# Attention and feed-forward on one core: early queries and keys loaded with two heads side by side, and the first sixteen weight loads cut in four

## The chip, the core and the metric

The kernel runs on one core of one Trainium2 chip. A core has TensorE (PE in the profile, PEld for its weight loads), VectorE (DVE), ScalarE (ACT), GpSimd (POOL) and SyncE (SP), each with an instruction queue of its own that is worked off in order. SyncE and, in a few places, ScalarE issue transfers (DMA) between the chip's memory and the core's SBUF. The metric is device time of one execution in microseconds.

## The reference

Eight batches of eight heads, 576 positions of 64 numbers each. Heads 0 to 3 look at the last 32 positions ("local"), heads 4 to 7 at every 32nd earlier position ("strided"). The attention's output goes through a feed-forward part with a gate.

```python
scores = scale * np.matmul(q, k.transpose(0, 1, 3, 2))
mask_local = (rel >= 0) & (rel < 32)
mask_strided = (rel >= 0) & (pos[None, :] % 32 == pos[:, None] % 32)
# softmax of the masked scores over the last axis
attn_out = np.matmul(attn, v)
x = attn_out.transpose(0, 2, 1, 3).reshape(4608, 512)
h = x @ w_in                                  # 512 x 2048
g = h * np.clip(h + 3.0, 0.0, 6.0) / 6.0
out = g @ w_out                               # 2048 x 512
```

Queries, keys and values are 32-bit floats, the two weight matrices 64-bit.

## The kernel before

The work is cut into tiles of 512 tokens, one for each batch `b`. Attention goes by pairs of heads: `pair(g)` does pair `c` of batch `b`, where pairs 0 and 1 are local and 2 and 3 strided; in the first batch the order is 0, 2, 1, 3. A pair has these steps: load queries and keys; turn them so that the 64 numbers of a head lie on the partitions (two heads on 128); scores in PSUM; mask, maximum, exponential, sum and division on the other engines; turn the result; multiply it with the values; copy it out as two parts of the tile's `x`. Then `ffn(b)` runs the two products of the feed-forward part, with each matrix split into a high and a low part, so that each product is three.

All of this is not issued as it is written. Each step is given to `op(engine, us, ...)` with a supposed duration, the data it reads and writes and a due time, and `Plan.emit` plays the steps through with these durations and writes the engines' instructions in the order that comes out. The durations are the planner's own numbers; a change to one moves instructions in the whole program. For loads, `after` is the time that the planner lets each take of the transfer's time. Where TensorE would have nothing to do for long early on, the planner puts in products without a use (`idle`), which keep it going.

The first four pairs (`early`, and those are what the change touches) load queries and keys in pieces that are contiguous in memory, and turn them on TensorE against the identity `ident`, one head at a time, by `upright`. In the profile the loaded tiles are `qn` and `kn`, the turned ones in PSUM `qp` and `kp` (the digits behind are pair and half), the copies in SBUF `qplain`, `kplain` or `qt`, `kt`, the scores `ps`, the turned results `pe`, and the products with the values `pv`. TensorE does a product of 32-bit floats in two passes, and the profile counts them, so 12 products show as x24.

`weight_part` loads one of 32 parts of the weights (128 rows of 512 numbers of 64 bits, 512 KB, `rawi` of w_in and `rawo` of w_out) and turns it into 32-bit floats from its bits: ScalarE L281 and L285, VectorE L289, then the high part on ScalarE (L303) or GpSimd (L305) and the low part on GpSimd (L308). The first sixteen (`k < 16`) are loaded while the first batch's attention runs.

Every load waits until the load that was issued eight before it has landed, since eight completion semaphores (`DMAHW0` to `DMAHW7`) are used in turn, SyncE's and ScalarE's loads counted together in the planner's order. So at most eight loads are under way, and a load that waits holds up all behind it on its queue.

Of the kernel before, what the change touches and what calls it, by code (L numbers as in the profile page):

```python
# [19 lines left out]
P = 128  # L20
# [9 lines left out]
TOK = 512  # L30
TURNS = ((0, 2, 1, 3), (2, 0, 3, 1)) + ((0, 2, 1, 3),) * 6
AHEAD = 27.0
OPEN = 6.0
HIENG = {"ACT": 0.63, "POOL": 0.7}

# [138 lines left out]
def attention_ffn(ctx: ExitStack, tc, q, k, v, w_in, w_out, out):  # L174
# [25 lines left out]
    def new(pool, key, shape, dtype, name):  # L200

        tag = "_".join(str(x) for x in key)
        t = tiles[key] = pool.tile(shape, dtype, tag=tag, name=name)
        return t
# [55 lines left out]
    def weight_part(k, w, g, i):  # L260
        key = wkey(w, g, i)
        fc = FQ * g if w == "i" else FQ * g + i + 1
        due = T0 + fc * TILE / NFC - 5.0 + 0.01 * k
        fkey = ("x", 1, 1 - (k // 2 % 2 if k < 20 else 0), k % 2)
        name = f"{w}{g}{i}"

        def load():
            if w == "i":
                src = w_in[i * P:(i + 1) * P, g * TOK:(g + 1) * TOK]
            else:  # L270
                src = w_out[(g * FQ + i) * P:(g * FQ + i + 1) * P, :]
            raw = new(wp, key, [P, TOK, 2], I32, f"raw{name}")
            nc.sync.dma_start(raw, src.bitcast(I32).rearrange("p (n t) -> p n t", t=2))

        def bits():
            raw = tiles[key]
            return raw.rearrange("p n t -> p (n t)")[:, :TOK]

        def high():
            f = new(xp, fkey, [P, TOK], I32, f"f{name}")  # L280
            nc.scalar.activation(f.bitcast(F32), tiles[key][:, :, 1].bitcast(F32), AF.Prelu, scale=2.0 ** -112, alpha=2.0 ** 32)  # L281

        def low():
            raw = tiles[key].bitcast(U16).rearrange("p n (t u) -> p n t u", u=2)[:, :, 0, 1]
            nc.scalar.activation(bits(), raw, AF.Copy, scale=2.0 ** -13, bias=2.0 ** -14 - 0.5)  # L285

        def join():
            f = tiles[fkey]
            nc.vector.scalar_tensor_tensor(out=f, in0=f, scalar=3, in1=bits(),  # L289
                                           op0=ALU.logical_shift_left, op1=ALU.bitwise_or)  # L290

        def whole():
            f = tiles[fkey].bitcast(F32)
            return f if w == "i" else f.rearrange("p (h e d) -> p h d e", h=2, d=2)

        def part(x):
            t = tiles[key][:, x]
            return t if w == "i" else t.rearrange("p (h d e) -> p h d e", h=2, d=2)

        def hi(e):  # L300
            new(wp, key, [P, 2, TOK], F32R, f"w{name}")
            if e == "ACT":
                nc.scalar.copy(part(0), whole())  # L303
            else:
                nc.gpsimd.tensor_copy(part(0), whole())  # L305

        def lo():
            nc.gpsimd.tensor_tensor(out=part(1), in0=whole(), in1=part(0).bitcast(F32), op=ALU.subtract)  # L308

        op("SP", 0.53, load, writes=[key], due=-49 + 0.01 * k if k < 4 else -48.4 + 0.01 * k if k < 6 else -2 + 0.1 * k if k < 16 else due - 20.0, early=7.0 if k < 16 else due - 30.0, after=1.6 if k < 16 else 1.25)  # L310
        op("ACT", 0.68, high, reads=[key], writes=[fkey], due=due - 5, room=LATE + 1.0)
        op("ACT", 0.68, low, writes=[key], due=due - 5)
        op("DVE", 1.05, join, reads=[key], writes=[fkey], due=due - 3)
        op(HIENG, 0, hi, reads=[fkey], writes=[key], due=due - 2)
        op("POOL", 1.3, lo, reads=[fkey, key], writes=[key + ("lo",), key], due=due - 1)
# [124 lines left out]
    def pair(g):  # L440
# [37 lines left out]
        for x in "qk":  # L478
# [6 lines left out]
            if early:  # L485
# [1 line left out]
                rows, ni = (QB, NQB) if loc else (S // 8, 8)  # L487

                def load(x=x, nkey=nkey, rows=rows, ni=ni):
                    t = new(wp, nkey, [P, 2, ni * D], F32, f"{x}n{nm}")  # L490
                    (nc.scalar if g < 2 and x == "k" else nc.sync).dma_start(
                        t[:rows], {"q": q, "k": k}[x][b, h0:h0 + 2].rearrange("j (p i) d -> p j (i d)", i=ni))
                tb = [slot(early) for _ in range(2)]

                def tr(x=x, nkey=nkey, tb=tb, rows=rows, ni=ni):
                    ps = [psum(tb[h], f"{x}p{nm}{h}") for h in range(2)]
                    half = ni // 2
                    for i in range(ni):
                        for j in range(2):
                            upright(ps[i // half], j, i % half * rows, tiles[nkey][:rows, j, D * i:D * i + D])  # L500

                def evac(e, x=x, tb=tb, h=0):
                    ps, to = tiles[tb[h].key][:, :S // 2], qk_of(x)
# [9 lines left out]
                        nc.scalar.copy(to, ps)  # L513
                    else:
                        nc.vector.tensor_copy(to, ps)
                op("ACT" if g < 2 and x == "k" else "SP", 0.55, load, writes=[nkey], due=-60 + 2 * g + (x == "k") - 900 * (g < 2 and x == "k"), after=1.15)
                op("PE", 0.13 * ni * slow, tr, reads=[("ident",), nkey, "plain"], writes=tb, take=tb, due=due - 1020, mode="s")
                for h in range(2):
                    op({"ACT": 0.45, "DVE": 0.4} if loc else {"ACT": 0.65, "DVE": 0.65}, 0, partial(evac, h=h), reads=[tb[h]],
                       writes=[tkey[x]] if h == 0 else [(tkey[x], 1)], give=tb[h], due=due - 19)  # L520
# [1083 lines left out]
```

## Time and profile before

| | |
|---|---|
| median of 3 runs | 870.39 us (869.03 to 871.68) |
| the profiled execution | 871.98 us, its span 870.2 |
| TensorE busy | 847.4 us, 97% of the span |
| weight loads on TensorE | 683.8 us, 79% |
| VectorE, ScalarE, GpSimd busy | 539.0, 558.9, 616.6 us (62, 64, 71%) |
| moved by DMA | 179.12 MB, 206 GB/s on average |
| granted TensorE clock, mean | 0.993 |

The span is the time from the first to the last instruction of the one execution that the profiler recorded. A row of the timeline gives the start in us, the length, the engine, the line, the operation and "out<-in"; xN is the number of instructions that were merged into it; in brackets stands the idle time before it, and what ended it. "issue" means that nothing which the profile shows was waited for. A matmul's length holds its way through the array, so that the starts of rows, not their lengths, tell the pace.

### The profile page before, as it was taken

To read this page: it belongs to the slowest core of one execution; us is meant where nothing else is said; L and a number is where in the kernel's file an instruction comes from. 1 tells how busy PE (TensorE), PEld (TensorE's weight loads), DVE (VectorE), ACT (ScalarE), POOL (GpSimd) and SP (SyncE) were. 2 spreads that over 40 slices of the span, in tenths; PEclk is the share of its full clock that TensorE was granted. 3 is DMA by queue.
4 is the path that set the end of the run, shared out by engine and by line. 5 is a ranking of instruction groups with operands and counts; after the bars stand their busy time and mean duration, and the time that the engine had idled before them with its cause. 6 is when DMAs were issued, how large, how long until landed. Compare 5 with 4: busy or idle time off the path is not lost.

```text
span 870.2 us, 18946 instructions
## 1 busy us (share of the span) xinstructions
PE 847.4 (97%) x6962; PEld 683.8 (79%) x6962; DVE 539.0 (62%) x898; ACT 558.9 (64%) x1246; POOL 616.6 (71%) x606
## 2 busy tenths in 40 slices
PE   8889999999999999999999999999999999999996
PEld 6667777887888788888888878788888778888884
DVE  5688878344454538454546664466767888555586
ACT  3687657678778865877677965776744645454441
POOL 4688877587547799766676994465975987767673
PEclk9999999999999999999999999999999999999998
DMA  8968723898984455898999897877666667866636
GB/s 194 330 138 233 234 41 73 210 281 245 279 234 108 128 129 141 233 266 233 269 277 289 274 301 214 237 204 189 183 202 193 185 180 222 240 202 192 183 122 145
DMA packets 323308, 179.12 MB, mean 206 GB/s; under 512 B 182864, under 2 KB 300368, under 8 KB 323216
## 3 DMA queue, kind: packets, MB, share of 16 engines
q1 hardware_dynamic: 318564, 176.27, 71.5%
q10 hardware_dynamic: 4652, 1.64, 0.9%
q8 instruction: 55, 0.90, 0.4%
q14 instruction: 37, 0.30, 0.1%
HBM read 136.97 MB, written 40.89 MB: 204 GB/s over the span
## 4 chain that ended last, share of the span: by engine, by line
PE 82%; DMA 5%; POOL 5%; DVE 4%; ACT 2%; issue 1%; SPq 0%; POOLq 0%; DVEq 0%; ACTq 0%
PE P L1129 8%; PE P L1130 8%; PE P L1131 8%; PE cP L1452 5%; PE cP L1453 5%; PE cP L1454 5%; PE acc L833 5%; PE ph L856 5%; PE ph L857 4%; PE ph L858 4%; PE acc L835 4%; PE acc L834 4%; PE acc L1214 3%; PE acc L1215 3%; PE acc L1216 3%; PE pv L399 2%
## 5 line engine op out<-in xcount | busy, mean ns | idle before, releaser
L1470 DVE SCALAR_TENSOR_TENSOR C<-cP,C 128x512 f32<-128x512 f32 x96 | 65.7, 687 | 40.4 <-PE cP L1454 39.5
L794 POOL TENSOR_TENSOR gl<-u,gh 128x512 fp32r<-128x512 f32 x48 | 65.2, 1361 | 33.3 <-ACT gh L790 17.1
L1141 DVE TENSOR_TENSOR G<-P,G 128x512 f32<-128x512 f32 x64 | 44.0, 689 | 65.6 <-PE P L1131 53.2
L1129 PE MATMUL P<-B_T,wr 128*128 128x512 f32 x192 | 76.1, 396 | 3.9 <-ACT G L1136 2.3
L833 PE MATMUL acc<-wo,gh 128*128 128x512 f32 x192 | 77.2, 402 | 0.0
L835 PE MATMUL acc<-wo,gl 128*128 128x512 f32 x192 | 75.2, 392 | 0.3 <-POOL gl L794 0.2
L834 PE MATMUL acc<-wo,gh 128*128 128x512 f32 x192 | 74.9, 390 | 0.0
L1130 PE MATMUL P<-B_T,wr 128*128 128x512 f32 x192 | 74.8, 390 | 0.0
L1131 PE MATMUL P<-B_T,wr 128*128 128x512 f32 x192 | 74.8, 390 | 0.0
L1136 ACT COPY G<-P 128x512 f32<-128x512 f32 x64 | 37.6, 587 | 52.2 <-PE P L1131 51.7
L1367 POOL TENSOR_TENSOR sp<-G,sp 128x512 fp32r<-128x512 f32 x34 | 47.6, 1411 | 24.6 <-ACT sp L1363 22.5
L665 POOL TENSOR_TENSOR e<-e,st 128x144 f32<-128x144 f32 (+1 forms) x64 | 44.9, 704 | 20.7 <-DVE st L661 15.2
L779 DVE SCALAR_TENSOR_TENSOR u<-u,ph 128x512 f32<-128x512 f32 x48 | 32.8, 684 | 38.0 <-ACT u L776 37.8
L856 PE MATMUL ph<-x,wi 128*128 128x512 f32 x128 | 52.5, 410 | 2.3 <-ACT x L426 1.2
L857 PE MATMUL ph<-x,wi 128*128 128x512 f32 x128 | 50.8, 397 | 1.4 <-DVE x L429 0.8
L700 ACT COPY atloc<-e 32x192 f32<-32x192 f32 x144 | 50.8, 353 | 1.9 <-DVE e L690 0.3
L776 ACT ACTIVATE u<-ph,three 128x512 f32<-128x512 f32 x48 | 33.0, 687 | 28.1 <-PE ph L858 27.8
L858 PE MATMUL ph<-x,wi 128*128 128x512 f32 x128 | 50.8, 397 | 0.0
L644 DVE TENSOR_REDUCE st<-e 128x8 f32<-128x144 f32 (+1 forms) x64 | 25.6, 412 | 35.8 <-POOL e L640 35.6
L1129 PE MATMUL P<-B_B,wr 128*128 128x512 f32 x120 | 47.1, 392 | 0.0
L1130 PE MATMUL P<-B_B,wr 128*128 128x512 f32 x120 | 46.8, 390 | 0.0
L1129 PEld LDWEIGHTS P<-B_T,wr 128*128 128x128 f32 x192 | 36.0, 188 | 13.7 <-ACT G L1136 3.6
(604 smaller groups left out, 2672.6 us busy)
## 6 DMA issues: line engine op xcount, KB each, us to landing
wr<-dA SPq DMA_DIRECT2D x72, 256.0 KB
or<-do SPq DMA_DIRECT2D x32, 512.0 KB
wr<-dSu SPq DMA_DIRECT2D x48, 256.0 KB
wr<-dSv SPq DMA_DIRECT2D x48, 256.0 KB
or<-do SPq DMA_DIRECT2D x48, 256.0 KB
rawi<-in_moe_w_in_dram SPq DMA_DIRECT2D x16, 512.0 KB
rawo<-in_moe_w_out_dram SPq DMA_DIRECT2D x16, 512.0 KB
do<-wo SPq DMA_DIRECT2D x16, 512.0 KB
```

Of the source, the lines that this page charges most:

```text
L700: nc.scalar.copy(at[PAD * (a + h):PAD * (a + h) + PAD, :, rows], e[rows, :, PAD * h:PAD * h + PAD])
L794: (nc.vector if tail else nc.gpsimd).tensor_tensor(out=to, in0=src(), in1=tiles[gk[0]].bitcast(F32), op=ALU.subtract)
L833: nc.tensor.matmul(acc, gh, woh, start=fc == 0, stop=False)
L834: nc.tensor.matmul(acc, gh, wol, start=False, stop=False)
L835: nc.tensor.matmul(acc, gl, woh, start=False, stop=end)
L856: nc.tensor.matmul(ph, wih, xh, start=n_ == 0, stop=False)
L857: nc.tensor.matmul(ph, wih, xl, start=False, stop=False)
L858: nc.tensor.matmul(ph, wil, xh, start=False, stop=n_ == NCC - 1)
L1129: nc.tensor.matmul(ph, wh, xh, start=fresh and k == 0, stop=False, skip_group_check=not fresh)
L1130: nc.tensor.matmul(ph, wh, xl, start=False, stop=False, skip_group_check=not fresh)
L1131: nc.tensor.matmul(ph, wl, xh, start=False, stop=k == 1, skip_group_check=not fresh)
L1470: nc.vector.scalar_tensor_tensor(out=tiles[ck], in0=tiles[bank], scalar=1.0 / 6.0, in1=tiles[ck], op0=ALU.mult, op1=ALU.add)
```

## The change

For the early pairs the two heads of a query or key load are put side by side in SBUF, so that each of the 6 or 8 slices `i` has 128 columns, 64 of each head. That takes one transfer per head, of pieces of 64 numbers (256 bytes). One product against the identity then turns a slice for both heads, where there were two. The first sixteen weight loads are issued as four transfers of 32 rows each. The planner's durations for these steps are new: 1.3 us of the issuing engine instead of 0.55 for a query or key load, 0.11 instead of 0.13 per slice for the turn, 1.6 instead of 0.53 for a weight load.

```diff
+CHOP = 4
...
             raw = new(wp, key, [P, TOK, 2], I32, f"raw{name}")
-            nc.sync.dma_start(raw, src.bitcast(I32).rearrange("p (n t) -> p n t", t=2))
+            step = P // CHOP if k < 16 else P
+            for p0 in range(0, P, step):
+                nc.sync.dma_start(raw[p0:p0 + step], src[p0:p0 + step].bitcast(I32).rearrange("p (n t) -> p n t", t=2))
...
-        op("SP", 0.53, load, writes=[key], ...)
+        op("SP", 0.4 * CHOP if k < 16 else 0.53, load, writes=[key], ...)
...
-                    t = new(wp, nkey, [P, 2, ni * D], F32, f"{x}n{nm}")
-                    (nc.scalar if g < 2 and x == "k" else nc.sync).dma_start(
-                        t[:rows], {"q": q, "k": k}[x][b, h0:h0 + 2].rearrange("j (p i) d -> p j (i d)", i=ni))
+                    t = new(wp, nkey, [P, ni, 2, D], F32, f"{x}n{nm}")
+                    for j in range(2):
+                        (nc.scalar if g < 2 and x == "k" else nc.sync).dma_start(
+                            t[:rows, :, j], {"q": q, "k": k}[x][b, h0 + j].rearrange("(p i) d -> p i d", i=ni))
...
-                        for j in range(2):
-                            upright(ps[i // half], j, i % half * rows, tiles[nkey][:rows, j, D * i:D * i + D])
+                        c0 = i % half * rows
+                        nc.tensor.matmul(ps[i // half][:, c0:c0 + rows], tiles[nkey][:rows, i].rearrange("p j d -> p (j d)"),
+                                         tiles["ident",][:rows, :rows], start=True, stop=True)
...
-                op(... "SP", 0.55, load, ..., after=1.15)
-                op("PE", 0.13 * ni * slow, tr, ...)
+                op(... "SP", 1.3, load, ..., after=1.3)
+                op("PE", 0.11 * ni * slow, tr, ...)
```

Where instructions stand changes on every engine. On TensorE, at the start of the real work, before (the turns of pair 0 and of pair 2, then pair 0's scores):

```order
L371 MATMUL qp_00_274<-ident,qn_0_134 64x96 [waits DMAHW1_49]
L371 MATMUL kp_00_297<-ident,kn_0_136 64x96 [waits DMAHW0_49]
L371 MATMUL qp_20_313<-ident,qn_2_186 64x72 [waits DMAHW3_49,DVE_49]
L371 MATMUL kp_20_337<-ident,kn_2_188 64x72 [waits DMAHW2_49]
L371 MATMUL kp_21_338<-ident,kn_2_188 64x72 x8
L608 MATMUL ps_00_361<-kplain,qplain 32x64 [waits DVE_49,Activation_49,Pool_49]
```

and in the changed kernel, up to the scores of pair 2 (`ps_20`):

```order
L504 MATMUL qp_00_273<-ident,qn_0_134 128x96 [waits DMAHW3_49,DMAHW1_49]
L504 MATMUL kp_00_286<-ident,kn_0_137 128x96 [waits DMAHW2_49,DMAHW0_49]
L504 MATMUL qp_20_301<-ident,qn_2_231 128x72 [waits DMAHW7_49,DMAHW5_49,DVE_49]
L613 MATMUL ps_00_317<-kplain,qplain 32x64 [waits DVE_49,Activation_49,Pool_49]
L504 MATMUL kp_20_357<-ident,kn_2_234 128x72 [waits DMAHW6_49,DMAHW4_49,DVE_49]
L504 MATMUL qp_10_377<-ident,qn_1_245 128x96 [waits DMAHW1_49,DMAHW0_49]
L504 MATMUL kp_10_394<-ident,kn_1_265 128x96 [waits DMAHW3_49,DMAHW2_49,Activation_49]
L605 MATMUL ps_20_405<-kplain,qplain 64x36 [waits Activation_49,Pool_49]
```

Pair 0's scores (L608, now L613) have moved ahead of the turn of pair 2's keys, and the `idle` product that stood between the turns of pair 1's queries and keys is gone. On SyncE, behind the query and key loads, before (values of pair 0, of pair 2, then the weights; `v_00` and `v_01` are pair 0's):

```order
L380 DMA v_01_239<-in_v_dram 64x9x64 [waits DMAHW5_49]
L566 DMA v_2_242<-in_v_dram 18x2x512 [waits DMAHW6_49,DVE_49]
L273 DMA rawi_333<-in_moe_w_in_dram 128x1024 [waits DMAHW2_49]
L273 DMA rawi_335<-in_moe_w_in_dram 128x1024 [waits DMAHW3_49]
L377 DMA v_10_260<-in_v_dram 32x64 [waits DMAHW6_49]
```

and in the changed kernel:

```order
L383 DMA v_01_239<-in_v_dram 64x9x64 [waits DMAHW5_49]
L276 DMA rawi_370<-in_moe_w_in_dram 32x1024 [waits DMAHW6_49]
L276 DMA rawi_370<-in_moe_w_in_dram 32x1024 [waits DMAHW7_49]
L276 DMA rawi_466<-in_moe_w_in_dram 32x1024 [waits DMAHW5_49]
L571 DMA v_2_242<-in_v_dram 18x2x512 [waits DMAHW6_49,DVE_49]
L380 DMA v_10_253<-in_v_dram 32x64 [waits DMAHW2_49]
```

Rows between these are left out where they only go on with the same load. The values of pair 2 have moved from ahead of the first four weights to behind them, and those are now sixteen transfers; the remaining weights follow behind the values of pairs 1 and 3, as before.

More of the change, by code (lines that the diff above doesn't have):

```diff
@@ L308, in lo @@
             nc.gpsimd.tensor_tensor(out=part(1), in0=whole(), in1=part(0).bitcast(F32), op=ALU.subtract)
-        op("SP", 0.53, load, writes=[key], due=-49 + 0.01 * k if k < 4 else -48.4 + 0.01 * k if k < 6 else -2 + 0.1 * k if k < 16 else due - 20.0, early=7.0 if k < 16 else due - 30.0, after=1.6 if k < 16 else 1.25)
+        op("SP", 0.4 * CHOP if k < 16 else 0.53, load, writes=[key], due=-49 + 0.01 * k if k < 4 else -48.4 + 0.01 * k if k < 6 else -2 + 0.1 * k if k < 16 else due - 20.0, early=7.0 if k < 16 else due - 30.0, after=1.6 if k < 16 else 1.25)
         op("ACT", 0.68, high, reads=[key], writes=[fkey], due=due - 5, room=LATE + 1.0)
@@ L515, in evac @@
                         nc.vector.tensor_copy(to, ps)
-                op("ACT" if g < 2 and x == "k" else "SP", 0.55, load, writes=[nkey], due=-60 + 2 * g + (x == "k") - 900 * (g < 2 and x == "k"), after=1.15)
-                op("PE", 0.13 * ni * slow, tr, reads=[("ident",), nkey, "plain"], writes=tb, take=tb, due=due - 1020, mode="s")
+                op("ACT" if g < 2 and x == "k" else "SP", 1.3, load, writes=[nkey], due=-60 + 2 * g + (x == "k") - 900 * (g < 2 and x == "k"), after=1.3)
+                op("PE", 0.11 * ni * slow, tr, reads=[("ident",), nkey, "plain"], writes=tb, take=tb, due=due - 1020, mode="s")
                 for h in range(2):
```

## The prediction

> **What bounds the kernel now.** I read the time by stage first, then the first 60 us instruction by instruction, then what SyncE's queue waits for. The stages (length; busy time of each engine; granted clock; DMA share and rate):
>
> ```profile
> 8.30:12.40 4.10, 4.10 (x113) 4.05 (x112) 2.16 (x4) 1.75 (x3) 0.00 (x0) 1.00 0.85 192
> 22.00:27.00 5.00, 2.90 (x41) 2.57 (x42) 3.23 (x9) 1.37 (x5) 2.39 (x5) 0.79 1.08 308
> 39.00:45.00 6.00, 5.61 (x97) 4.17 (x98) 4.05 (x9) 4.72 (x11) 6.00 (x11) 1.00 1.03 415
> 50.00:60.00 10.00, 8.31 (x55) 6.03 (x54) 7.48 (x11) 8.20 (x16) 8.42 (x7) 0.83 0.49 98
> 60.00:100.00 40.00, 39.45 (x407) 30.76 (x405) 34.78 (x65) 29.30 (x53) 36.17 (x32) 1.00 0.75 213
> 140.00:870.20 730.20, 717.55 (x5247) 582.75 (x5245) 433.50 (x684) 469.52 (x1070) 512.34 (x485) 1.00 0.74 210
> ```
>
> From 60 us on TensorE is busy 39.45 of 40 us, and from 140 us 717.55 of 730.2: there it is the bound, and the change leaves its work alone. So the change can only move the moment at which TensorE gets going, and that is decided in the first 60 us. The instructions there (start, length, engine, line, what ended the idle time before):
>
> ```profile
> 8.30 1.21 PE L371 MATMUL qp<-ident,qn 96*64 96x96 f32 x24
> 9.34 1.16 PE L371 MATMUL kp<-ident,kn 96*64 96x96 f32 x24
> 11.33 1.17 PE L371 MATMUL kp<-ident,kn 72*64 72x72 f32 x32
> 10.55 0.68 ACT L513 COPY kplain<-kp 128x288 f32<-128x288 f32 x1 [0.32 <-PE kp L371]
> 12.43 0.97 PE L608 MATMUL ps<-kplain,qplain 64*32 64x64 f32 x72
> 14.47 0.91 PE L1570 MATMUL idle<-ident 128*128 128x384 f32 x2
> 15.32 1.21 PE L371 MATMUL kp<-ident,kn 96*64 96x96 f32 x24
> 18.16 1.02 PE L600 MATMUL ps<-kplain,qplain 64*64 64x36 f32 x55 [1.34 <-issue]
> 19.21 1.12 ACT L626 COPY e<-ps 32x144 f32<-32x144 f32 x4 [1.66 <-PE ps L600]
> 24.83 2.14 PE L371 MATMUL pe<-ident,e 96*64 96x96 f32 x19 [2.10 <-issue]
> 26.89 1.52 PE L608 MATMUL ps<-kt,qt 64*32 64x64 f32 x72
> 38.03 0.93 PE L371 MATMUL pe<-ident,e 96*64 96x96 f32 x12
> 38.90 0.50 PE L856 MATMUL ph<-x,wi 128*128 128x512 f32 x1
> ```
>
> The first product of the feed-forward part comes at 38.90. Before it lies a chain of short steps of four pairs of heads: turn queries and keys (qp, kp), copy, scores (ps), softmax on the other engines, turn, values. TensorE runs without a gap from 8.30 to 13.40, and the scores of pair 0 (12.43) stand behind the turning of pair 2's keys (11.33). The scores of pair 2 end at 19.18, and ScalarE waited 1.66 us for them. Between 22.7 and 28.4 lie an idle time of 2.10 us that the profile puts on no engine, and a clock of 0.79.
>
> **The profiled run** took 871.98 us, its span being 870.2. The median of the runs shown is 870.39, 1.59 below it; I work out a difference in the trace and subtract it from the median.
>
> **Loads of queries and keys.** Eight loads, so far 4 of 192 pieces (96 rows x 2 heads) and 4 of 144, 1,344 in all, become sixteen with 8 x 1,152 = 9,216 pieces of 256 bytes (96 x 6 or 72 x 8, twice). Windows with nearly nothing but 256-byte pieces show the price: in this order 14 to 15 us, 26 to 27 us, 54 to 56 us, and, for 4 KB pieces, 32 to 36 us.
>
> ```profile
> DMA packets 574, 0.15 MB, mean 152 GB/s; under 512 B 567, under 2 KB 567, under 8 KB 574
> DMA packets 1036, 0.26 MB, mean 262 GB/s; under 512 B 1034, under 2 KB 1034, under 8 KB 1036
> DMA packets 1396, 0.40 MB, mean 199 GB/s; under 512 B 1367, under 2 KB 1367, under 8 KB 1396
> DMA packets 413, 1.52 MB, mean 379 GB/s; under 512 B 47, under 2 KB 47, under 8 KB 411
> ```
>
> That is 574, 1,036 and 698 pieces per us, so 16.1, 8.9 or 13.2 us for all. I take 698: that row holds loads over all 128 partitions, and the new loads, over 96 and 72, are nearest to it. Flow starts near 2.8 us: from 2 to 6 us, in slices of 0.1, the rate is
>
> ```profile
> GB/s 92 108 15 31 15 31 123 138 200 230 184 276 307 338 445 384 384 415 384 420 307 266 271 328 236 277 236 236 236 236 164 312 317 302 282 312 302 277 266 287
> ```
>
> Then the last key lands at 16.0 (bounds 11.7 and 18.9), and pair 1's keys, the sixth of eight, at 12.7 (9.5 to 14.9). Before, SyncE's queue shows it, since every load waits for the one issued eight before it:
>
> ```profile
> 0.73 1.27 SPq L491 DMA_DIRECT2D qn<-in_q_dram  x3
> 5.72 0.33 SPq L377 DMA_DIRECT2D v<-in_v_dram  x1
> 12.81 1.02 SPq L380 DMA_DIRECT2D v<-in_v_dram  x1
> 14.15 2.48 SPq L566 DMA_DIRECT2D v<-in_v_dram  x4
> SPq L566 <- DMA kn<-in_k_dram: 1.1, 1, 1.1
> 16.95 2.10 SPq L273 DMA_DIRECT2D rawi<-in_moe_w_in_dram  x4
> ```
>
> Pair 0's keys had landed at 5.72, pair 1's at 12.81, and pair 3's near 15.6 (14.15, one issue of 0.33, then 1.1 of waiting). So the loads end where they ended: 0 us, bounds 0 to +0.5 (worked out below). Pair 0 (2 of 8 loads) needs to be there at 8.30, when the warm-up products end; it lands between 5.0 and 6.8. Of the eight more issues two are on ScalarE's queue, which has nothing to copy before TensorE's first turn, and six on SyncE's, in front of the value loads, whose first use is at 28.34.
>
> **One product for both heads.** Six products of three and three instead of twelve per load; in the trace 12 passes instead of 24, each with 128 stationary columns instead of 64. The beat is now 1.02/24 = 43 ns. The loads of weights into TensorE, 64 columns above (least, median and most ns), 128 below (busy us, mean ns):
>
> ```profile
> L371 PEld LDWEIGHTS qp<-ident,qn x112: 132/137/138, 8.3 to 20.0; 72*64 72x64 f32 x64, 96*64 96x64 f32 x48
> L1129 PEld LDWEIGHTS P<-B_T,wr 128*128 128x128 f32 x192 | 36.0, 188 | 13.7 <-ACT G L1136 3.6
> ```
>
> Sixty-four more columns take 51 ns more, so a load of 128 goes on for some 102 ns at that rate. If the passes follow at the old beat, a turn costs 12 x 43 = 0.5 us; if each waits for its weights, 12 x 102 = 1.2 us. Now it is 1.0 (the starts 8.30, 9.34, 11.33). I take 1.0, no gain, because in a stream that is half weight loads their row is the nearest. The Trainium skill, in "TensorE: Matmul & The Clock Gate", section "LDWEIGHTS (loading the stationary operand)", gives the load's time as columns divided by 1.2 per ns; that is 107 ns for 128, the 51 ns above agree, and it speaks against a halving: by it alone a turn would be 1.28 us and the scores of pair 0 would come at 12.1.
>
> **Order on TensorE.** The turning of pair 2's keys now stands behind the scores of pair 0. These start after three turns, 8.30 + 3 x 1.0 = 11.3 instead of 12.43. Bounds: 12.0 with turns of 1.2; 10.4 with turns of 0.5, since ScalarE's last copy of the keys, 0.68, must be through. Then scores 1.0, and three turns (keys 2, queries 1, keys 1, without the fill of 0.91 at 14.47) end at 15.3; pair 1's keys are there at 12.7. A copy that must first free a bank, 0.68, may hold them that long once. Pair 2's scores so start at 15.3 to 16.0 instead of 16.5, where the turning at 15.32 ended. If the idle time of 1.34 in their middle stays, they end about 0.9 earlier, at 18.3. Slowest end: turns of 1.2, or keys at 14.9, give 15.9 to 16.7, a gain of 0.5 to a loss of 0.2. Fastest: turns of 0.5 and keys at 9.5 give 13.4, a gain of 3. What is late next is ScalarE's copy at 19.21, and from there on every engine has the rows it had; I carry 0.9 us through to 38.90.
>
> **First sixteen weights in four parts.** 48 more issues on SyncE. Sixteen loads are 8.39 MB, 22.1 us at 379 GB/s. With the shortest issue, 0.33 and 0.04 between two, 64 take 23.7 us: the last lands some 1.5 us later, if nothing else changes. Pair 2's values are issued behind the first four weights, before it was ahead of them. The uses:
>
> ```profile
> 27.30 0.68 ACT L281 ACTIVATE fi<-rawi 128x512 f32<-128x512 f32 x1
> 28.34 0.77 PE L388 MATMUL pv<-at,v 64*64 64x32 f32 x36
> 32.26 1.22 PE L735 MATMUL pv<-atstr,v 128*64 128x72 f32 x32
> 38.77 9.25 SPq L357 DMA_DIRECT2D qn<-in_q_dram  x4
> 59.17 1.36 DVE L533 STREAM_TRANSPOSE qplain<-qn 128x576 f32<-128x576 f32 x1
> 62.34 0.66 ACT L281 ACTIVATE fo<-rawo 128x512 f32<-128x512 f32 x1
> ```
>
> By the middle rate, pair 0's values (2,240 pieces) land near 16.0 + 3.2 = 19.2, and its use is 28.34. The first weight lands near 20.7 (1.4 us a weight), its use is 27.30: ScalarE's queue, not the load, sets that. Pair 2's values land near 26, use 32.26. The thirteenth weight lands well before 62.34. Cost 0; the cover is 6 us or more each, and it is gone only if the rate falls (third rival).
>
> **Sum:** 0 + 0 - 0.9 + 0, rounded to -1.0 with a little of the fill saved: 870.39 - 1.0 = 869.4.
>
> **Rivals.** *Larger gain.* Turns take 0.5 us (3 us at pair 2's scores), or the stretch of 22.7 to 28.4 dissolves: its 2.10 us of idle time, and the slow clock after it, 2.14 for 19 passes against 0.93 for 12 (0.7 us) and 1.52 against 0.97 (0.55 us), together 3.3. Either gives about 3.5: 866.9. For it: the slow clock follows the idle time; against it: nothing in the change aims at that wait.
>
> *Absorbed.* Between 39 and 60 GpSimd, ScalarE and VectorE turn weights and softmax at 75 to 100% (6.00 of 6; 8.20 of 10), and TensorE waits for them:
>
> ```profile
> 53.76 0.50 PE L856 MATMUL ph<-x,wi 128*128 128x512 f32 x1 [1.20 <-ACT x L426]
> ```
>
> If their queues set the pace there, starting earlier gives nothing: 870.4. Later rows have another order too, in both directions, which I cannot price.
>
> *Slower.* Parts of 32 partitions move at half the rate, 190 GB/s. Sixteen weights then take 44 us instead of 22 and end near 66 with the values between them, instead of 47 to 48 (the loads at 38.77 waited until then). The second tile's queries, which VectorE turns at 59.17, are issued behind the last weight. VectorE stands near 5 us with joins of weights behind it, and TensorE has some 2 us of ready products: 870.4 + 3 = 873.4. The point from which it decides is a rate under some 230 GB/s, at which the weights end at 57. For it: no load of 32 partitions with long pieces is in this trace. Against it: four parts of one load, at other partitions, are in flight at once. The Trainium skill, in "SBUF — State Buffer", section "Door 1: The DMA port swizzle (why [64,N] ≈ [32,N])", says that the rate depends on how many of 16 ports the partitions reach, which for 32 are 8; that rule would make the time this rival's, and no row here shows it.
>
> **How the numbers follow.** 0.3%, 2.6 us, is about what a measurement tells from no change. Chances: the sum 0.33, larger gain 0.29, absorbed 0.21, slower 0.17. Larger gain lies mostly beyond 2.6 us with one end at 3.5, the slow rival at 3; so faster 0.28, same 0.55, slower 0.17. The range 865.5 to 872.6 takes in both bounds of the turns and half of the slow rival; the sum's own is 867.9 to 870.6.
>
> **What would show it.** Right: pair 0's scores near 11.3, pair 2's ending near 18.3, first feed-forward product near 37.9, TensorE from 100 us on as before. Turns: 1.0 us each if the weight load sets the beat, 0.5 if not. Wrong: pair 1's keys turned after 15 us; weights landing at under 250 GB/s, with VectorE waiting for the second tile's queries near 60; or the first feed-forward product earlier and the row of 50 to 60 us emptier by as much.

## The result, and the profile after

The changed kernel takes 880.69 us (median of 6 runs, 879.64 to 885.20) beside 871.30 us for the kernel before (6 runs, 869.03 to 874.27): a ratio of 1.0121, 95% interval 1.0101 to 1.0140, so about 9.4 us slower. The profiled execution took 881.06 us, its span being 879.3; before it was 871.98 and 870.2.

The stages of the changed kernel, in the columns of the table in the prediction (length; busy time of each engine; granted clock; DMA share and rate):

```profile
22.00:27.00 5.00, 5.00 (x45) 4.00 (x46) 2.80 (x11) 2.65 (x9) 3.55 (x7) 1.00 0.85 223
39.00:45.00 6.00, 5.56 (x96) 3.90 (x96) 3.57 (x9) 4.19 (x11) 6.00 (x11) 1.00 0.99 240
50.00:60.00 10.00, 7.99 (x36) 5.41 (x33) 5.90 (x10) 9.57 (x19) 9.61 (x8) 1.00 1.03 241
60.00:100.00 40.00, 33.69 (x355) 26.36 (x354) 32.38 (x55) 24.69 (x46) 29.84 (x29) 0.94 0.91 211
140.00:879.30 739.30, 725.23 (x5280) 589.08 (x5278) 443.14 (x702) 473.37 (x1076) 515.38 (x490) 1.00 0.74 208
```

From 39 to 45 us the DMA engines are as busy as before (0.99 and 1.03) and move 240 GB/s where they moved 415; from 50 to 60, where before they had work for 0.49 of the time, they are still full (1.03). From 60 to 100 us TensorE is busy 33.69 of 40 us, where it was 39.45, and runs at a clock of 0.94 on top. Early on, the stretch of 22 to 27 us has no idle time and a full clock, where before it had 2.90 of 5 and 0.79. The first steps on TensorE (start, length, engine, line; L504 is the turn, L613 pair 0's scores, L861 the first product of the feed-forward part):

```profile
9.37 1.48 PE L504 MATMUL qp<-ident,qn 96*128 96x96 f32 x12
10.69 1.50 PE L504 MATMUL kp<-ident,kn 96*128 96x96 f32 x12
12.03 1.93 PE L504 MATMUL qp<-ident,qn 72*128 72x72 f32 x16
13.88 0.97 PE L613 MATMUL ps<-kplain,qplain 64*32 64x64 f32 x72
37.87 0.50 PE L861 MATMUL ph<-x,wi 128*128 128x512 f32 x1
```

A turn of 96 rows takes 1.32 us from start to start and one of 72 rows 1.85, where each took 1.0. Still the first product of the feed-forward part comes 1.0 us earlier than before. From the first turn to it are 28.5 us (37.87 - 9.37), where they were 30.6 (38.90 - 8.30). So the chain is 2.1 us shorter, and 1.1 of it are lost ahead of the chain: the same 14 warm-up products took longer in this execution. Before, and after:

```profile
2.79 5.58 PE L1570 MATMUL idle<-ident 128*128 128x384 f32 x14
2.87 6.67 PE L1575 MATMUL idle<-ident 128*128 128x384 f32 x14
```

SyncE's queue with the parts of the weights and the second tile's queries (L360), and who waits then:

```profile
15.72 9.03 SPq L276 DMA_DIRECT2D rawi<-in_moe_w_in_dram  x16
33.01 8.69 SPq L276 DMA_DIRECT2D rawo<-in_moe_w_out_dram  x16
41.74 8.86 SPq L276 DMA_DIRECT2D rawi<-in_moe_w_in_dram  x16
50.77 8.31 SPq L276 DMA_DIRECT2D rawo<-in_moe_w_out_dram  x16
59.37 1.95 SPq L360 DMA_DIRECT2D qn<-in_q_dram  x4
```

```profile
DVE qplain L538 <- DMA vstr<-in_v_dram: 4.2, 1, 4.2
PE ph L861 <- DVE u L784: 2.8, 2, 2.0
PE ps L613 <- DVE kplain L538: 2.5, 1, 2.5
```

The second tile's queries are issued at 59.37 instead of 38.77. VectorE, which turns them (L538), stands 4.2 us (one wait), and TensorE 2.5 us for its keys. (The row names the load of `vstr` as what ended the wait. By the row of the operation it reads `qn`, and `vstr` was issued only at 64.15, 0.65 us before the wait ended; that it was the queries' load is inferred.) That is the mechanism of the prediction's third rival. It is not the whole loss, as the experiments show.

### The profile page after: what moved, and what is told of

The parts are those of the page before. It is cut to its first block, busy times and chain, and to the rows that moved or that the text cites. A ratio compares the mean times of both kernels' runs of the same rounds, so it can differ in the third digit from the quotient of the medians.

```text
span 879.3 us, 18855 instructions
## 1 busy us (share of the span) xinstructions
PE 851.9 (97%) x6850; PEld 688.2 (78%) x6850; DVE 543.5 (62%) x900; ACT 556.6 (63%) x1242; POOL 611.6 (70%) x608
## 4 chain that ended last, share of the span: by engine, by line
PE 81%; POOL 5%; DVE 4%; DMA 4%; SPq 3%; issue 1%; ACT 1%; ACTq 0%; POOLq 0%; DVEq 0%
PE P L1134 9%; PE P L1136 8%; PE P L1135 8%; PE cP L1457 5%; PE cP L1459 5%; PE cP L1458 5%; PE acc L838 5%; PE acc L840 5%; PE acc L839 4%; PE ph L861 4%; PE ph L863 4%; PE ph L862 4%; PE acc L1219 3%; PE acc L1221 3%; PE acc L1220 3%; DMA rawi<-in_moe_w_in_dram 2%
## 5 line engine op out<-in xcount | busy, mean ns | idle before, releaser
L838 PE MATMUL acc<-wo,gh 128*128 128x512 f32 x192 | 78.3, 408 | 0.7 <-POOL wo L311 0.7
L839 PE MATMUL acc<-wo,gh 128*128 128x512 f32 x192 | 75.8, 395 | 0.6 <-POOL wo L311 0.6
L670 POOL TENSOR_TENSOR e<-e,st 128x144 f32<-128x144 f32 (+1 forms) x64 | 43.0, 675 | 19.1 <-DVE st L666 16.2
L861 PE MATMUL ph<-x,wi 128*128 128x512 f32 x128 | 51.9, 405 | 3.9 <-DVE u L784 3.6
L863 PE MATMUL ph<-x,wi 128*128 128x512 f32 x128 | 50.2, 392 | 2.0 <-POOL wi L311 2.0
L862 PE MATMUL ph<-x,wi 128*128 128x512 f32 x128 | 50.1, 391 | 0.4 <-DVE x L432 0.4
L1134 PE MATMUL P<-B_B,wr 128*128 128x512 f32 x120 | 47.7, 398 | 0.1
L1135 PE MATMUL P<-B_B,wr 128*128 128x512 f32 x120 | 46.8, 390 | 0.0
L1136 PE MATMUL P<-B_B,wr 128*128 128x512 f32 x120 | 46.8, 390 | 0.0
L1134 PEld LDWEIGHTS P<-B_T,wr 128*128 128x128 f32 x192 | 36.0, 188 | 11.3 <-DVE G L1146 2.0
L840 PEld LDWEIGHTS acc<-wo,gl 128*128 128x128 f32 x192 | 36.6, 190 | 10.6 <-POOL gl L799 2.7
```

Of the source, the lines that this page charges most:

```text
L838: nc.tensor.matmul(acc, gh, woh, start=fc == 0, stop=False)
L839: nc.tensor.matmul(acc, gh, wol, start=False, stop=False)
L840: nc.tensor.matmul(acc, gl, woh, start=False, stop=end)
L861: nc.tensor.matmul(ph, wih, xh, start=n_ == 0, stop=False)
L862: nc.tensor.matmul(ph, wih, xl, start=False, stop=False)
L863: nc.tensor.matmul(ph, wil, xh, start=False, stop=n_ == NCC - 1)
```

## The experiments

Four theories stood at the start. A: a part over 32 adjacent partitions moves slowly, because of the partitions that it writes. B: each issue has a price, so that 64 are slow whatever they write. C: the planner's new numbers put the work into a worse order. D: the new loads and turns themselves cost time. Each ratio is to the kernel before, measured in the same set of runs. To place a loss in the profiled execution I use one row of each trace, the products of the feed-forward part with `xh` and `wi`, which gives its last start, and the first start of the row `ph<-x,wi`. Of before and after (count; least, median and most ns; first to last start):

```profile
L856 PE MATMUL ph<-x,wi x128: 387/389/632, 38.9 to 250.4; 128*128 128x512 f32 x128
L856 PE MATMUL ph<-xh,wi x64: 389/389/500, 253.1 to 351.4; 128*128 128x512 f32 x64
```

```profile
L861 PE MATMUL ph<-x,wi x128: 387/389/504, 37.9 to 259.5; 128*128 128x512 f32 x128
L861 PE MATMUL ph<-xh,wi x64: 389/389/499, 261.5 to 359.6; 128*128 128x512 f32 x64
```

From 38.9 to 351.4 are 312.5 us before, from 37.9 to 359.6 are 321.7 after: the loss lies in this stretch, and it is 9.2 us. The same numbers for the kernels below, in the order of telling. The stretch is that of one execution and the time a median. What lies behind the stretch differs too: in two kernels of the table that turn out to have the same instructions in the same order (whole weights, and queries and keys alone) 518.6 and 523.0 us pass from the last start to the end. So a few us of stretch and of median need not agree.

| kernel | first | last | stretch | median us | ratio, interval |
|---|---|---|---|---|---|
| before | 38.9 | 351.4 | 312.5 | 871.3 | |
| changed | 37.9 | 359.6 | 321.7 | 880.7 | 1.0121 (1.0101-1.0140) |
| whole weights | 37.8 | 354.2 | 316.4 | 875.7 | 1.0052 (1.0027-1.0076) |
| cut alone | 35.9 | 357.3 | 321.4 | 877.5 | 1.0070 (1.0046-1.0094) |
| two adjacent halves | 36.5 | 358.4 | 321.9 | 880.1 | 1.0118 (1.0078-1.0158) |
| two interleaved halves | 36.7 | 354.4 | 317.7 | 876.6 | 1.0061 (1.0042-1.0081) |
| four interleaved parts | 37.5 | 365.6 | 328.1 | 890.3 | 1.0213 (1.0175-1.0251) |
| four column parts | 37.0 | 358.6 | 321.6 | 881.0 | 1.0110 (1.0090-1.0131) |
| queries and keys alone | 37.8 | 354.3 | 316.5 | 876.7 | 1.0069 (1.0049-1.0089) |
| order alone | 34.5 | 353.0 | 318.5 | 878.3 | 1.0089 (1.0061-1.0117) |
| load number alone | 36.9 | 352.0 | 315.1 | 879.7 | 1.0092 (1.0066-1.0118) |
| turn number alone | 41.0 | 368.1 | 327.1 | 890.0 | 1.0210 (1.0195-1.0225) |
| new forms, old order | 47.6 | 359.5 | 311.9 | 879.7 | 1.0067 (1.0039-1.0095) |
| two products, old order | 37.1 | 348.6 | 311.5 | 870.5 | 0.9994 (0.9983-1.0004) |
| two products, new order | 39.5 | 355.5 | 316.0 | 877.4 | 1.0080 (1.0060-1.0099) |
| short joins, order alone | 42.0 | 354.0 | 312.0 | 877.3 | 1.0072 (1.0046-1.0098) |
| short joins, old order | 37.8 | 351.6 | 313.8 | 870.4 | 0.9995 (0.9979-1.0011) |
| joins held back | 35.8 | 358.5 | 322.7 | 880.6 | 1.0118 (1.0096-1.0140) |
| short joins, one product | 36.4 | 350.8 | 314.4 | 873.7 | 1.0020 (1.0003-1.0038) |

**The cut of the weights, taken out and done alone.** From the changed kernel, with the planner's numbers kept:

```diff
-            step = P // CHOP if k < 16 else P
+            step = P
```

> Changed kernel with the first sixteen weights loaded whole again (128 partitions a load), everything else, the planner's costs and so the order of all other instructions, as changed. Theory A (a part over 32 adjacent partitions moves at the rate of half the partitions' ways in, 240 GB/s): the rate from 16 us on goes back to 370-415 GB/s, the last weight lands near 48 us, the second tile's loads are issued before 45, the time is 868.5-871.5. Theory B (each issue or each small transfer has a fixed price, whichever partitions it writes): the same numbers. Theory C (the planner's new cost moved other work to worse places): the rate returns, but the time stays at 878-882. Theory D (the queries and keys, their 256-byte pieces and 128-column turns): 878-882, with the rate back.

875.69 us. The rate is back (36 to 46 us), the second tile's queries are issued at 41.08, and half of the loss stays:

```profile
DMA packets 1114, 4.07 MB, mean 407 GB/s; under 512 B 125, under 2 KB 125, under 8 KB 1111
```

```profile
41.08 7.31 SPq L360 DMA_DIRECT2D qn<-in_q_dram  x4
```

The other way round, the kernel before with only the cut (`step` as in the change, and the planner's 1.6):

> Kernel before with only the weights cut in four (and the planner's cost for them), queries and keys as before. Theories A and B: 235-260 GB/s, last weight at 58-61 us, 878-882 us, or about 1 us more than the changed kernel if the gain of the early attention was the queries' and keys'. Theory C: 876-882 with the slow rate or without. Theory D: 869-872.

877.54 us. Its issues show what the changed kernel's do, and behind VectorE's 7.0 us for those loads TensorE stood 6.19 us:

```profile
59.26 2.14 SPq L360 DMA_DIRECT2D qn<-in_q_dram  x4
```

```profile
DVE qplain L536 <- DMA vstr<-in_v_dram: 7.0, 1, 7.0
```

```profile
68.53 0.79 PE L836 MATMUL acc<-wo,gh 128*128 128x512 f32 x1 [6.19 <-DVE u L782]
```

So the cut costs 5.9 us in the old order (877.54 to 871.69). In the new one, with each kernel compared with the kernel before of its own set, it costs 5.4 (9.4 less the 4.0 of whole weights); by the second measurement of the kernel without it, below, 3.7 (9.4 less 5.7). The rest, 4.0 to 5.7 us, is of another part.

**Partitions or issues.** Parts over every fourth partition, with as many issues and as many 4 KB pieces:

```diff
+            step = CHOP if k < 16 else 1
+            for p0 in range(step):
+                nc.sync.dma_start(raw[p0::step], src[p0::step]...)
```

> Changed kernel with each of the four parts over every fourth partition (0, 4, 8 ... and so on) in place of 32 adjacent ones: as many issues, as many pieces of 4 KB, the same bytes and the same order. Theory A (which partitions a part reaches): 350-415 GB/s and 868.5-872 us. Theory B (a fixed price of each issue): 235-260 GB/s as with adjacent parts, and 878-882 us. Theory C (order) and D (queries and keys): rate up, time 878-882.

890.25 us, neither theory's number. The rate (46 to 66 us) is 203 GB/s, but the DMA engines have work for only 0.70 of the time, and SyncE waits for no transfer; sixteen issues take 10.44 us, 0.65 each:

```profile
DMA packets 1486, 4.07 MB, mean 203 GB/s; under 512 B 495, under 2 KB 495, under 8 KB 1485
q1 hardware_dynamic: 1485, 4.06, 69.9%
```

```profile
46.35 10.44 SPq L276 DMA_DIRECT2D rawi<-in_moe_w_in_dram  x16
```

There the issue is the bound, 128 KB in 0.65 us. Two halves of 64 partitions halve the number of issues and so make that bound looser. Adjacent first (`step = P // 2`):

> Changed kernel with two parts of 64 adjacent partitions in place of four of 32, the order as changed. Theory A, in the form that the Trainium skill gives it in SBUF - State Buffer, section Door 1: The DMA port swizzle, by which 64 adjacent partitions reach no more ports than 32: 235-260 GB/s, 878-882 us. Theory B (fixed price of an issue; 8.7 us for 16 issues of 32 partitions against 5.4 for four whole loads' bytes): the price halves, 300-320 GB/s, last weight near 53 us, 872-876 us. C and D: 878-882 at a higher rate.

then every second partition (`raw[p0::2]`):

> Changed kernel with two parts of 64 partitions each, every second one (even, odd), in place of four of 32. As many issues and pieces as the two adjacent halves, which went at 245 GB/s and gave 880. An issue over stepped partitions took 0.59 us, so the queue can hand out 256 KB in 0.6 us, 430 GB/s, and is no bound. Theory A (which partitions a part reaches): 330-400 GB/s, the second tile's first queries issued before 48 us, 874-877 us, as with whole weights. Theory B (the number of issues): 240-260 GB/s and 878-882.

The transfers of both, adjacent (39 to 55 us) and interleaved (38 to 48 us):

```profile
DMA packets 1182, 3.89 MB, mean 243 GB/s; under 512 B 236, under 2 KB 236, under 8 KB 1180
q1 hardware_dynamic: 1180, 3.87, 102.6%
```

```profile
DMA packets 1109, 3.66 MB, mean 366 GB/s; under 512 B 220, under 2 KB 220, under 8 KB 1106
q1 hardware_dynamic: 1106, 3.63, 99.8%
```

With as many issues and pieces, and engines full in both, 64 adjacent partitions take the data at 243 GB/s and 64 spread ones at 366, and 876.63 us is the time of whole weights again (875.7 and 876.7). The 366 may still be a little low: eight of these issues took 5.70 us, with at most 0.8 of waiting for a transfer. 64 adjacent partitions are no faster than 32 (238 to 241 GB/s). The spread halves also read every second row of the weights from memory, where adjacent ones read one contiguous stretch. Whole weights read contiguously as well, at 407 GB/s, so that alone is not slow, but no run changes one side without the other. With this left open it is theory A, and it agrees with the Trainium skill, "SBUF — State Buffer", section "Door 1: The DMA port swizzle (why `[64,N]` ≈ `[32,N]`)", which lets partitions 0 to 31 and 0 to 63 reach the same 8 of 16 ports.

Theory B holds too, a little further on. Four parts by columns, over all partitions, in pieces of 1 KB:

```diff
+            step = TOK // CHOP if k < 16 else TOK
+            for c0 in range(0, TOK, step):
+                nc.sync.dma_start(raw[:, c0:c0 + step], ...)
```

> Changed kernel with four parts by columns, each over all 128 partitions in pieces of 1 KB, in place of 32 partitions in pieces of 4 KB: as many issues and bytes. Theory A (partitions): above 300 GB/s and 874-877 us, unless the shorter pieces take it away: at 128 pieces an issue and the some 1,000 short pieces per us of the early loads, no less than 260 GB/s would be left for pieces of 1 KB, 877-880. Theory B (issues): 235-260 GB/s, 878-882.

```profile
DMA packets 4318, 3.96 MB, mean 247 GB/s; under 512 B 476, under 2 KB 4316, under 8 KB 4316
q1 hardware_dynamic: 4316, 3.93, 80.8%
```

```profile
42.36 9.16 SPq L276 DMA_DIRECT2D rawi<-in_moe_w_in_dram  x16
```

880.98 us: the engines are not full (0.81), SyncE waits for no transfer, and an issue takes 9.16/16 = 0.57 us. (The 1 KB pieces may cost as well: at 0.81 for 247, full engines would have given some 305, an estimate.) So four parts were slow in each of three forms, by the partitions (adjacent) or by the issues (the two others). TensorE's wait for the second tile's keys, behind 60 us, goes with it: none with whole weights and with spread halves, 2.5 us in the changed kernel and with columns, 3.9 with adjacent halves, 9.7 with four interleaved parts, which issue these queries only at 67.08.

**The other half: forms or order.** The kernel before with the change of queries and keys alone:

> Kernel before with only the queries' and keys' loads and turns changed, and the planner's numbers for these alone; the weights whole, at the cost that they had. The kernel with whole weights but the planner's new cost for them took 875.7, 4.0 over before. Theory D (the side-by-side loads and 128-column turns themselves cost time): 874-877. Theory C (the weights' new cost in the planner, 1.6 for 0.53, moved later work): 869-872, with TensorE's wait of 2.0 us for VectorE's u in 80-100 us gone. An even split would give 873.

876.73 us. The planner's number for the weights turned out to move no instruction, with either form of the queries and keys. So this kernel does the same in the same order as the one with whole weights, and is its second measurement; theory C's reading of that number falls, and its other numbers remain. Then all four planner numbers, with the old loads, turns and whole weights:

```diff
-0.55, load, ... after=1.15    -0.13 * ni * slow, tr    -0.53, load
+1.3, load, ... after=1.3      +0.11 * ni * slow, tr    +0.4 * CHOP if k < 16 else 0.53, load
```

> Kernel before, its loads, products and weights in their old form, with all four planner numbers of the change (weights 1.6, queries and keys 1.3 and 1.3, turns 0.11 a slice): its engines do the work in the changed kernel's order. Theory C (order): 874-877, with TensorE's wait of about 2 us for u between 80 and 100 us. Theory D (form of the loads and turns): 869-872.

878.33 us, with nothing new but the order. In the profiled execution (875.19, the fastest of six) TensorE reaches the feed-forward part at 34.5, 4.4 us earlier than before, and its last product of the stretch at 353.0, 1.6 later: 6.0 us are lost on the way. Two single numbers confirm that the deal of the order is worth that much, in the kernel before with 1.3 for a load's cost, and with 0.11 for a turn's:

> Kernel before with a single other planner number changed, the queries' and keys' load cost of 1.3 for 0.55; forms and weights as before. The turns keep the order of before, later rows do not. Order theory: again 2 us or more either way, 866-878, with the early stretch as before. If orders are worth little: 869-873.

> Kernel before with a single planner number changed, the turn's cost of 0.11 for 0.13 a slice; forms and weights as before. The order is dealt anew from the first turns on (pair 2's keys behind pair 0's scores) and differs in 27 to 140 places of each engine's table. Order theory: not the work but the deal decides, so a change of 2 us or more either way, 865-878, with the first feed-forward product some 3 us earlier as in the order-alone run and the difference made between 60 and 120 us. If orders are worth little: 869-873.

879.68 and 889.97 us. The second, which changes 0.13 into 0.11 and nothing else, loses 18.5 us, more than was expected of any order. In its trace TensorE is idle for 9.0 of the 80 us from 100 to 180, where before it was for 0.8, and its clock is 0.94; no run took these waits away.

The forms themselves, in the old order (the planner's numbers of before, whole weights), with one product and with two of 64 columns:

> Side-by-side loads and one product for both heads, with whole weights and the planner's old numbers, so that every engine keeps the order of before. Order theory (the loss of 4.0 to 5.7 us of the queries-and-keys part alone is the re-dealt order, since order alone without the new forms cost 7.3): 869.5-872.5. Form theory (turns of 1.3 and 1.9 us instead of 1.0, 4.8 us more TensorE time in the first 27 us, of which the 3.4 us idle there can take a part): four turns stand ahead of pair 0's scores, which come 2.5 to 3 us later than before, the first feed-forward product at 40-42, 872.5-875.

> As the run of the new forms in the old order, but with two products of 64 columns a slice, as before, read from the side-by-side layout. Form theory: turns back at 1.0 us, so 2.5 to 3 us earlier at pair 0's scores than with one product; 869.5-872. If the turns' length is hidden anyway, or the loads are what costs, it equals the run with one product within 1 us.

The side-by-side load with two products is 870.53 us, 0.9994 of before: 256-byte pieces in eight more transfers cost nothing. One product costs 9 us there by the median, but most of that is not the length of its turns. Between 14 and 15 us TensorE's granted clock falls to 0.50 and stays there until 41; three windows of that kernel, with the columns of the stages:

```profile
12.00:14.00 2.00, 2.00 (x20) 2.00 (x20) 0.67 (x2) 0.40 (x1) 0.00 (x0) 1.00 0.76 171
14.00:16.00 2.00, 2.00 (x78) 1.76 (x77) 0.15 (x1) 0.40 (x1) 0.00 (x0) 0.64 0.64 145
22.00:27.00 5.00, 5.00 (x79) 4.76 (x79) 1.25 (x4) 3.35 (x10) 1.27 (x2) 0.50 1.02 323
```

No idle time shows there. Four of its seven executions had a mean clock of 0.982 to 0.983 and took 879.7 to 880.7, three had 0.995 to 0.998 and took 872.4 to 875.0, which is 0.9 to 3.6 over the 871.46 of the kernel before, so that the interval in the table, 1.0039 to 1.0095, is of two kinds mixed. The changed kernel had a clock of 1.00 through that time. The same pair in the new order:

> New order, side-by-side loads, whole weights, two products of 64 columns a slice. With one product the same kernel took 875.7 and 876.7; in the old order one product took 879.7 and two 870.5. If the product's form costs by its slow clock alone, which was not seen in the new order (mean clock 0.992 to 0.997): 875-878.5, no better than one product. If the longer turns cost in any order: 870-873.

877.36 us with two products, 875.7 and 876.7 with one: there one product costs nothing. Its mean clocks are even the better ones, 0.992 to 0.997 against 0.987 to 0.989 with two. So theory D falls, and the half of the loss that isn't the cut is theory C, the order, 7.0 us with two products and 4.0 to 5.7 with one.

**Where the order loses.** In the order-alone kernel TensorE waits at 88.97 for VectorE's `u` (L780 there, L779 before), and its clock falls behind that. Windows of order alone, then of before:

```profile
85.00:90.00 5.00, 3.03 (x14) 2.17 (x12) 4.90 (x12) 2.45 (x6) 5.00 (x5) 1.00 1.00 378
90.00:95.00 5.00, 3.99 (x11) 2.83 (x10) 4.96 (x8) 4.70 (x10) 4.38 (x5) 0.53 0.80 235
95.00:100.00 5.00, 5.00 (x19) 4.01 (x18) 4.94 (x6) 0.66 (x1) 3.38 (x3) 0.79 0.01 2
```

```profile
85.00:90.00 5.00, 5.00 (x24) 4.14 (x23) 4.58 (x11) 3.86 (x8) 4.79 (x4) 1.00 0.97 327
90.00:95.00 5.00, 4.79 (x22) 3.63 (x21) 4.50 (x7) 2.64 (x5) 4.68 (x5) 1.00 0.91 365
95.00:100.00 5.00, 4.73 (x43) 3.50 (x41) 4.74 (x7) 3.86 (x6) 4.04 (x3) 1.00 0.21 38
```

`u` is the gate's product of the feed-forward part, and a join is the step on VectorE that puts a weight together from two pieces of its bits (L289 before). VectorE is busy 14.8 of 15 us, and in its new order three joins stand ahead of that `u`, between it and the `u` of the chunk before, where the old order has one. The three were cut short to 16 of 512 columns, with the other 496 left out, in that kernel and as a control in the one before:

```diff
+            if k in (15, 16, 17):
+                f, b_ = f[:, :16], b_[:, :16]
```

> The order-alone kernel with three joins (weights 16 to 18 in order) on 16 of 512 columns, the order unchanged; what it leaves out is the joining of three weights' halves in the other 496 columns, 2 to 5 us of VectorE. Joins theory: u comes 2 to 4 us earlier at 88 us, TensorE's wait of 2.0 us and the clock of 0.53 go, 871-874.5 against 878. Otherwise 876-880.

> Control: the kernel before with the same three joins on 16 columns. TensorE waits 0.3 us for u between 60 and 100 us there, so the saving of VectorE's time should be worth under 1 us: 869.5-871.5. If it falls by as much as the order-alone kernel does, the joins are a load on any order and not the mark of this one.

The control gained nothing (870.39). In the order-alone kernel the wait for `u` fell from 2.0 to 0.5, but the time only from 878.3 to 877.3, within the intervals: its profiled execution had a clock of 0.73 from 8 to 40 us and came to the feed-forward part at 42.0 instead of 34.5, so the two stretches can't be compared. Holding the joins back instead, which deals the rows behind them anew:

> The order-alone kernel with an earliest time for the joins of two weights, so that VectorE's u of the chunk stands ahead of them; rows before it are the same, rows after it are dealt anew. Joins theory (u behind three joins makes TensorE wait 2.0 + 1.0 us at 89 to 92 and run at clock 0.53 and 0.79 for 10 us after it): the wait goes, TensorE keeps most of the 4.4 us it is early, 867-873. If the loss sits in many places of the order: 875-880.

880.61 us, slower: the wait for `u` is gone, and one of 2.59 us for GpSimd's `gl` stands at 92.32 in its place. The short joins were then put into the kernel that starts at the same time in both its profiles, the one with whole weights and one product:

> The kernel with whole weights in the new order (one product for both heads), which took 875.7 and 876.7, with three joins (weights 16 to 18) on 16 of 512 columns; the joining of the other 496 columns is left out. Its first feed-forward product should come at 37.8 as there. Joins theory: TensorE's wait of 2.0 us for u goes, and with it the clock of 0.75 and 0.90 in the 10 us behind; from the first to the last product of the first feed-forward part 312 to 313 us in place of 316.4, 871-873.5. If the loss is spread over the order: 875-877.

873.69 us, 2.0 and 3.0 under the 875.7 and 876.7 without. Its stretch is 314.4 instead of 316.4, and the clock stays at 1.00 behind the wait, which is 0.6 instead of 2.0:

```profile
PE ph L863 <- DVE u L786: 0.6, 1, 0.6
```

```profile
90.00:95.00 5.00, 4.33 (x19) 3.11 (x19) 5.00 (x7) 4.11 (x9) 4.33 (x5) 1.00 1.00 395
```

So the joins ahead of `u` are about half of what the order costs there, by medians. The interval of this kernel lies clear of that of queries and keys alone and overlaps that of whole weights. That no join can be shortened without giving VectorE less work stays an objection; the control in the old order gained nothing from it. The other 2.2 us (873.7 to 871.5) are not placed. One piece is seen only in traces: between 500 and 530 us TensorE waited 1.7 to 3.6 us for a load (`or<-do`) in every kernel with all of the new order, and 0.4 before. No run takes this wait away.

## Why the prediction was wrong

The forecast was 869.4 in a range of 865.5 to 872.6; the result, 880.7, is on the other side and beyond the slow rival's 873.4. Point by point:

- **Weights in four parts, "8.39 MB at 379 GB/s", "Cost 0": the step that failed.** The rate was 238 to 241, the last part was issued at 59, with the working it would have landed near 49. The row used was one of loads over 128 partitions, taken for a load over 32. The third rival had the mechanism, and was too low twice. Its rate (190) was below what came, yet its "point from which it decides" (under some 230 GB/s, weights ending at 57) was passed at 238, because the parts were not issued in one stretch: 8.3 us lie between the first sixteen and the next. And its price, 3 us, was 4 to 6. TensorE had more than the "some 2 us of ready products" (VectorE stopped at 60.63, TensorE at 65.78), but its clock fell behind the wait (0.94 over 40 us), and no term stood for that. Its argument against, that parts at other partitions are in flight at once, is refuted by the two halves: 243 GB/s with several under way.
- **The order, "from there on every engine has the rows it had": failed as well, by 4.0 to 7.3 us.** A sentence in the second rival said that later rows have another order "which I cannot price", and the sum then took 0 for it. Order alone, 7.3 us, costs more than the cut alone, 5.9, and the planner's duration of a turn or of a load is enough by itself to cause a loss of this size.
- **Turns, 1.0 us taken: too low.** They took 1.32 and 1.85, which is 110 ns for each of 12 passes and 116 for each of 16. The rule of the Trainium skill that the prediction weighed there ("TensorE: Matmul & The Clock Gate", section "LDWEIGHTS (loading the stationary operand)"), 107 ns for 128 columns and so 1.28 us a turn, was nearer than the row that I chose: the pace is as if each pass waits for its weights. It did no harm to the time in the new order.
- **Queries and keys, 0: right** (0.9994 with two products), though by too low a rate. From 2 to 6 us 3,457 pieces landed and from 6 to 10 us 3,897, 864 and 974 per us where 698 were taken. By 12 us 8,287 of the 9,216 had landed, so the end came some 1.5 us behind that (an estimate, at the 552 to 705 per us then), and not at 16.0.
- **First feed-forward product near 37.9: the number came, the reason didn't.** Pair 0's scores came at 13.88, not 11.3, later than before, and 1.07 of that is the later start of the turns, for which the prediction had no term. With the chain shorter by 2.1 us and that start later by 1.1, the forecast 1.0 came by luck. In the kernels with this order of TensorE's instructions the turns started between 8.16 and 9.62, and what sets it is not shown. What was saved is the idle time and slow clock of 22.7 to 28.4, the second half of the first rival. And the gain was not carried: order alone started 4.4 us early and ended late.
- **What would show it.** "Weights landing at under 250 GB/s, with VectorE waiting for the second tile's queries near 60" is what the trace shows. "TensorE from 100 us on as before" nearly holds: from 100 to 140 us its clock was 0.97, and from 140 to 180 it was busy 39.45 of 40 us, where it was 40.00.

## What to carry to other kernels

Where a load is cut in parts, the parts should spread over the partitions, and the price of an issue decides how small they may be: here 64 adjacent partitions went at 243 GB/s, 64 spread ones at 366, and no form of four parts passed 247. Where a planner sets the order, a change of its numbers is a change of the whole program, and is to be measured alone before anything is said of the edit that came with it: one number, 0.13 to 0.11, was worth 18.5 us, and the turn that it was meant to describe cost nothing in the new order. A start that is 4 us earlier was worth nothing here, where an engine further on had work queued in front of what the bound engine needs.

## What the runs showed of the hardware that I had not expected

- The granted clock fell to 0.50 for 26 us with TensorE busy all the time by the profile, behind a stream of 128-column weight loads with one short product each (96 or 72 columns). In the old order four such turns stand in a row, 6.3 us; in the new one scores stand behind the third, and the clock stayed at 1.00. With two products of 64 columns in the old order all twelve executions had a mean clock of 0.991 to 0.996. The Trainium skill, "TensorE: Matmul & The Clock Gate", section "What's actually happening", has the gate follow how busy the array is; that such a stream counts as idle is my reading, and the runs show only when it happens. Nor does it need that stream: with short joins in the new order, where each turn is two products of 64 columns, the clock was 0.50 from 20 to 36 us as well, there behind 1.55 us of idle time between 16 and 20.
- The same 14 warm-up products took 5.52 to 7.08 us in the profiled executions of all these kernels, so that the start of the real work moved by over 1 us whatever was changed.
- A join over 16 columns took 2.90 us on VectorE. GpSimd was in an operation when it began (79.66 to 80.48) and had two more without a pause (80.44 to 82.99); the join ended within 0.03 us of the last. Of the kernel with short joins and one product, VectorE and GpSimd:

```profile
79.66 0.82 POOL L655 TENSOR_TENSOR e<-e,st 96x384 f32<-96x384 f32 x1
80.12 2.90 DVE L294 SCALAR_TENSOR_TENSOR fo<-fo,rawo 128x16 int32<-128x16 int32 x1
80.44 1.30 POOL L313 TENSOR_TENSOR wo<-fo,wo 128x512 fp32r<-128x512 f32 x1
81.70 1.29 POOL L801 TENSOR_TENSOR gl<-u,gh 128x512 fp32r<-128x512 f32 x1
```

  The shortest join of 16 columns took 0.125 us. The Trainium skill, "SBUF — State Buffer", section "SBUF: two separate sides", says that VectorE with two inputs from SBUF and a GpSimd operation that reads SBUF exclude each other for a whole instruction. The trace agrees, with the addition that the join was not let in between GpSimd's operations, and it explains why cutting 97% of a join saved only a part of its time.
- Four parts over every fourth partition took 0.65 us an issue and column parts 0.57, both without a wait for a transfer. The 0.55 of 32 adjacent partitions is the pace of their transfers (128 KB at 238 GB/s). That the step costs is not shown: the shortest issue was 0.47 us for 64 partitions, adjacent and spread alike, 0.49 for every fourth partition, 0.31 for 32 adjacent ones and 0.33 for columns.
